# The three-pass products of two MLP-style mixings: float32r parts replaced by scaled float16 parts, with a range check and a second path

## The chip, the cores and the metric

The kernel runs on one core of a Trainium2 chip. The metric is the device time of one execution in microseconds (us); lower is better. Three runs of the kernel before gave 607.79, 611.24 and 612.61 us, median 611.24 us. The profile that is read below is one further execution.

## The reference

`B, H, S, D = 2, 8, 768, 64`, so 1536 rows of 512 columns, in 12 tiles of 128 rows. Causal windowed attention (8 global keys, a window of 96, a distance bias) gives `x`; then two mixings follow. The MLP weights reach the kernel as float64.

```python
attn_out = _attn_ref(**attn_kwargs)                  # softmax(q k / 8 + bias, masked) v
x = ascontiguousarray(attn_out.transpose(0, 2, 1, 3)).reshape(B, S, H * D)
# first mixing: layer norm, 512 -> 2048 -> 512
xn = (x - mu) / np.sqrt(var + 1e-06) * g_ln
x = x + np.maximum(xn @ w_ch1, 0.0) @ w_ch2
# second mixing: along the 768 rows (768 -> 256 -> 768), then 512 -> 1536 -> 512
u = x + (np.maximum(x.transpose(0, 2, 1) @ w_tok1, 0.0) @ w_tok2).transpose(0, 2, 1)
out = u + np.maximum(u @ w_ch1, 0.0) @ w_ch2
```

## The kernel before

**Products in three passes.** Every product of the mixings is made from a high and a low part of each operand: `hi` is the operand rounded to the matmul's type (ScalarE, `hi_lo`, L312, or `Weights.split`, L630), `lo` is the rest (VectorE, L316 and L319, or GpSimd and VectorE, L633). `mm3` (L323 to L326) then adds hi·hi, hi·lo and lo·hi in PSUM. The parts are float32r, a 4-byte type; PSUM is float32. Matmuls of the attention itself use float32 and, from tile 6 on, 16-bit parts (`ph`, `pl` float16 against `vb` bfloat16, L449 to L451).

**Tiling.** Rows go in four groups of three tiles (`xa`, `xb`, `u`). A first-layer block (tile `L1`, shown as `L`) is 4 chunks of 128 rows of weights times 3 passes, 12 matmuls of 384 columns; a second-layer block (`L2`, `L2S`) adds 4 or 2 hidden blocks, 12 or 6 matmuls of 512 columns; the product along the rows (`tok1`, `tok2`) has 512 columns. In the later part the first layer uses a Strassen-like scheme (`Factors`, `summands`, `pair`): sums and differences of weights (`Q`, then split into `sz`) and of activations (`K`, `V`, then split into `t`, `u`) are made on VectorE and GpSimd, and seven products stand for eight.

**Weights.** `Weights.get` loads 512 KB of float64 words into `stg`, ScalarE makes the sign and exponent word `fw` (L603), VectorE joins it with the mantissa (L614) in PSUM (`conv`) or SBUF (`wf`), then the two parts are split. Weights of both mixings are stored split in device memory (`scr_...`, 512 KB each) and loaded again for later groups.

**Order.** All engines' programs are written out by a planner (`Plan.order`): each operation has an engine, a cost and a due time, and a simulated list scheduler gives the order; buffers are pools with fixed counts (`SIZES`). Tables of letters (`LOA1`, `SE`, `FE`, ...) say which engine does which low part or sum; tables of numbers (`SLOT`, `LEAD`, ...) shift due times.

**Branches and end.** `setup_consts` computes a flag (the two counts fit the windowed path, L84); every engine loads it (L1202) and branches: windowed path, or `Else` with the general path. Behind it SyncE stores the last two tiles (`BEHIND`, `store`, L934).

Of the kernel before, what the change touches and what calls it, by code (L numbers as in the profile page):

```python
# [22 lines left out]
P = 128  # L23
# [11 lines left out]

class Ctx:
# [3 lines left out]
def setup_consts(o, tp):  # L40
# [17 lines left out]
    for fw in o.fws:  # L58
        nc.gpsimd.memset(fw[:, :, 0], 0.0)
# [8 lines left out]
    nc.scalar.activation(out=warm[:], in_=o.mhalf, func=AF.Exp)  # L68

# [5 lines left out]
                                   op1=ALU.add)  # L75
    ps = o.nps.tile([P, 2], F32, name="nps")
# [3 lines left out]
    flag = cp.tile([1, 1], I32, name="flag")  # L80
# [3 lines left out]
    nc.vector.scalar_tensor_tensor(out=flag[:], in0=ng, scalar=float(NGF), in1=c2[:, 1:2], op0=ALU.is_le, op1=ALU.mult)  # L84
# [444 lines left out]
def norm_ops(o, plan, prio, T, grp, i):  # L529
# [4 lines left out]
    xn = Buf("xn", lambda: o.ln.tile([P, C], F32, tag="xn", name="xn", bufs=1))  # L534
# [32 lines left out]

class Weights:


    def __init__(self, o, plan, keep):
        self.o, self.plan, self.kept, self.keep = o, plan, set(), keep

    def get(self, src, prio):
# [3 lines left out]
        b = Buf(key, lambda: o.wp.tile([P, 2, 512], F32R, tag=key, name=key))  # L578
        if src in self.kept:
            op("S", 1.46, prio - RELOAD, lambda: o.nc.sync.dma_start(b.t[:].bitcast(F32), o.kept[src][:]), r=[("kept", src)],  # L580
               w=[(b, "h"), (b, "l")], get=[b])
            return b
        self.split(src, prio, lambda: (b.t[:, 0, :], b.t[:, 1, :]), (b,), [b])
        if src[0] in self.keep:
            def store():
                t = o.kept[src] = o.scr.tile([P, 2, 512], F32, name=f"scr_{src[0]}{src[1]}{src[2]}")
                o.nc.sync.dma_start(t[:], b.t[:].bitcast(F32))
            op("S", 1.46, prio + STORE, store, r=[(b, "h"), (b, "l")], w=[("kept", src)])
            self.kept.add(src)
        return b  # L590

    def split(self, src, prio, dst, key, get=(), r=(), after=()):
        o, nc, op = self.o, self.o.nc, self.plan.op
        engs = {(1, "a"): LOA1, (1, "b"): LOB1, (2, "a"): LOA2, (2, "b"): LOB2}.get(src[:2], LOT)
        lo_eng = engs[src[2]] if o.w64 else "G"
        stg = Buf("stg", lambda: next(o.stg))
        if o.w64:
            if src in o.staged:
                op("N", LOADED[src], -9.0 + 0.1 * src[2], lambda: None, w=[(stg, 0)], get=[stg])
# [3 lines left out]
            op("A", 0.57, prio - 2, lambda: nc.scalar.activation(  # L603
                out=fw.t[:, :, 1], in_=stg.t[:, 4:2049:4].bitcast(BF16), func=AF.Copy),
# [21 lines left out]
        def shaped():  # L626
# [24 lines left out]
class Factors:  # L651
# [4 lines left out]
    def __init__(self, o, plan, name, xs, tiles, prio, r=(), after=()):  # L656
# [5 lines left out]
        for j in range(2):  # L662
            sx = [Buf("sx", lambda: next(o.sx)) for _ in range(4)]

            for z, (x, kc, k) in enumerate(((xa, j, ka), (xb, j, kb), (xa, 2 + j, ka), (xb, 2 + j, kb))):
                self.sum(op, nc, FE[z], prio, lambda z=z, sx=sx: sx[z].t, lambda x=x, kc=kc: x()[:, 0, kc, :n].bitcast(F32),
                         lambda x=x, kc=kc: x()[:, 1, kc, :n].bitcast(F32), ALU.add, n, r=[*k, *r], w=[(sx[z], 0)], get=[sx[z]])
# [3 lines left out]
            for i, z in enumerate((0, 3, 1, 2)):  # L671
# [4 lines left out]
                         lambda i=i, j=j: self.tiles()[i][:, 0, j].bitcast(F32), ALU.subtract, n,  # L676
# [11 lines left out]
def mlp_ops(o, plan, W, groups, blocks, which, t0, stores=False, lead=8.0, factors=None):  # L688
# [18 lines left out]
    def hidden():  # L707
        return Buf("hid", lambda: o.hid.tile([P, 2, max(GROUPS) * P], F32R, tag="h", name="h"))

    def l1(bi, f, g):  # L710
# [12 lines left out]
        cost = 12 * (0.014 + n / 2400)  # L723
# [7 lines left out]
    def l2(bi, hs, fs, g, ti, end, use="L2"):  # L731
# [12 lines left out]
        op("T", 3 * len(fs) * 0.227, prio, fn, r=keys, w=[(b, 0)], get=[b])  # L744
# [4 lines left out]
        now[0] += 3 * len(fs) * 0.216  # L749

    def summands(bi, fs):
# [16 lines left out]
        for i in range(2):  # L768
# [4 lines left out]
                        lambda i=i: z[i].t[:, 0].bitcast(F32), ALU.subtract, 512, r=[*k, (z[i], "h")], w=[(z[i], "l")])  # L773
        return w, z

    def pair(bi, fs, gs, pending):
# [7 lines left out]
        cost = 6 * (0.014 + n / 2400)  # L784
# [79 lines left out]
def token_ops(o, plan, b, uT, prio):  # L864
# [388 lines left out]
```

## Time and profile before

| | |
|---|---|
| median of 3 runs | 611.24 us |
| profiled execution, own time | 609.82 us |
| its span (first to last instruction) | 607.8 us |
| TensorE matmul / weight load busy | 586.1 us (96%) / 516.8 us |
| VectorE / ScalarE / GpSimd busy | 451.7 / 255.5 / 160.4 us |
| moved by DMA | 118.54 MB, mean 195 GB/s |

Busy time of TensorE is modelled: a matmul's duration in the trace lasts until its result has left the array, so consecutive matmuls overlap, and what a stream costs is read from start to start, not from the mean duration. PEld is the weight load, a record of its own. The chain of waits tells which engine's work stood last at each moment.

### The profile page before, as it was taken

The numbers are of one execution on the slowest core, as the hardware profiler recorded it, in microseconds if no ns is written. First come the engines' busy times: TensorE is split into PE (matmuls) and PEld (weight loads), VectorE is DVE, ScalarE is ACT, GpSimd is POOL, SyncE is SP. The second block draws the span as 40 slices with busy tenths as digits, with TensorE's granted clock in tenths as the row PEclk, the third lists the DMA queues.
The fourth block names the chain that finished last, engine by engine and source line by source line (L and its number), as shares of the span: only waits on it lengthen the run. The fifth ranks groups of instructions, "written<-read, shape, count | busy, mean of one in ns | idle before, by whom it ended". The sixth has DMA issues, their size and how long they took to land.

```text
span 607.8 us, 9319 instructions
## 1 busy us (share of the span) xinstructions
PE 586.1 (96%) x3318; PEld 516.8 (85%) x3318; DVE 451.7 (74%) x974; ACT 255.5 (42%) x499; POOL 160.4 (26%) x159
## 2 busy tenths in 40 slices
PE   3989999999999899999999999999999999999997
PEld 3767988988988788999899988798999898999986
DVE  7777676677754687988778987685699999677642
ACT  5778663446444353454222444341645423222100
POOL 2324143111602323243112311023343224411000
PEclk9989999999999999999999999999999999999999
DMA  9879999778936512748433545020429757553241
GB/s 260 302 215 314 315 325 327 287 231 281 310 132 234 191 47 70 243 151 302 169 127 121 201 177 208 1 105 35 174 74 342 278 168 249 185 194 140 104 157 57
DMA packets 63403, 118.54 MB, mean 195 GB/s; under 512 B 21620, under 2 KB 35956, under 8 KB 63348
## 3 DMA queue, kind: packets, MB, share of 16 engines
q1 hardware_dynamic: 63346, 117.86, 57.0%
q8 instruction: 28, 0.46, 0.3%
q14 instruction: 27, 0.22, 0.1%
q10 hardware_dynamic: 2, 0.00, 0.0%
HBM read 84.93 MB, written 32.51 MB: 193 GB/s over the span
## 4 chain that ended last, share of the span: by engine, by line
PE 85%; DMA 4%; DVE 4%; ACT 3%; issue 1%; POOL 1%; SPq 0%; POOLq 0%; DVEq 0%; ACTq 0%
PE L L324 16%; PE L L326 16%; PE L L325 15%; PE L2S L324 7%; PE L2S L325 7%; PE L2S L326 7%; PE S L405 4%; PE T L431 3%; PE PV L436 2%; PE tok L324 2%; PE tok L326 2%; PE tok L325 2%; DMA stg<-in_moe_w_ch_dram 2%; DMA stg<-in_moe_w_tok_dram 1%; ACT fw L603 1%
## 5 line engine op out<-in xcount | busy, mean ns | idle before, releaser
L746 DVE TENSOR_TENSOR x<-L2S,x 128x512 f32<-128x512 f32 x93 | 63.8, 687 | 25.7 <-PE L2S L326 25.1
L324 PE MATMUL L2S<-wb,h 128*128 128x512 f32 x204 | 80.1, 393 | 1.0 <-DVE x L746 1.0
L326 PE MATMUL L2S<-wb,h 128*128 128x512 f32 x204 | 79.8, 391 | 0.0
L325 PE MATMUL L2S<-wb,h 128*128 128x512 f32 x204 | 79.8, 391 | 0.0
L603 ACT ACTIVATE fw<-stg 128x512 f16<-128x512 bf16 x62 | 49.0, 791 | 50.0 <-DMA stg<-in_moe_w_ch_dram 32.4
L316 DVE SCALAR_TENSOR_TENSOR h<-L,h 128x384 fp32r<-128x384 f32 x56 | 31.0, 554 | 30.3 <-ACT h L312 29.9
L324 PE MATMUL L<-wb,h 128*128 128x512 f32 x132 | 53.1, 403 | 0.0
L326 PE MATMUL L<-wb,h 128*128 128x512 f32 x132 | 51.7, 392 | 0.0
L325 PE MATMUL L<-wb,h 128*128 128x512 f32 x132 | 51.7, 391 | 0.0
L312 ACT ACTIVATE h<-L 128x384 fp32r<-128x384 f32 x56 | 27.4, 489 | 55.1 <-PE L L326 54.8
L426 ACT ACTIVATE ex<-ex,mn 128x256 f32<-128x256 f32 (+1 forms) x96 | 41.6, 482 | 18.6 <-DVE mn L421 18.5
L324 PE MATMUL L<-xa,wa 128*128 128x384 f32 x136 | 46.9, 345 | 0.0
L324 PEld LDWEIGHTS L2S<-wb,h 128*128 128x128 f32 x204 | 38.3, 188 | 9.3 <-DVE x L746 2.4
L326 PE MATMUL L<-xa,wa 128*128 128x384 f32 x136 | 45.7, 336 | 0.0
L746 DVE TENSOR_TENSOR x<-L,x 128x512 f32<-128x512 f32 x33 | 22.8, 690 | 30.9 <-PE L L326 30.7
L325 PE MATMUL L<-xa,wa 128*128 128x384 f32 x136 | 45.6, 336 | 0.0
L633 POOL TENSOR_TENSOR wb<-wf,wb 128x512 fp32r<-128x512 f32 x17 | 23.4, 1387 | 83.8 <-ACT wb L630 77.9
L326 PEld LDWEIGHTS L2S<-wb,h 128*128 128x128 f32 x204 | 38.3, 188 | 8.2
L325 PEld LDWEIGHTS L2S<-wb,h 128*128 128x128 f32 x204 | 38.4, 188 | 6.8
L421 DVE CUSTOM_DVE_ANT_0 ex<-bmh,S 128x256 f32<-128x256 bf16 (+1 forms) x96 | 34.0, 394 | 6.1 <-PE S L405 5.8
L312 ACT ACTIVATE h<-V 128x384 fp32r<-128x384 f32 x28 | 14.4, 523 | 55.0 <-DVE V L800 35.9
L633 POOL TENSOR_TENSOR wa<-wf,wa 128x512 fp32r<-128x512 f32 x14 | 18.7, 1333 | 66.9 <-ACT wa L630 65.3
(194 smaller groups left out, 1527.1 us busy)
## 6 DMA issues: line engine op xcount, KB each, us to landing
stg<-in_moe_w_ch_dram SPq DMA_DIRECT2D x56, 512.0 KB, 5.3
wa<-scr_1a SPq DMA_DIRECT2D x24, 512.0 KB, 4.3
wb<-scr_1b SPq DMA_DIRECT2D x24, 512.0 KB, 5.4
scr_1a<-wa SPq DMA_DIRECT2D x16, 512.0 KB, 4.1
scr_1b<-wb SPq DMA_DIRECT2D x16, 512.0 KB, 5.3
wa<-scr_2a SPq DMA_DIRECT2D x16, 512.0 KB, 3.5
wb<-scr_2b SPq DMA_DIRECT2D x16, 512.0 KB, 4.0
scr_2a<-wa SPq DMA_DIRECT2D x12, 512.0 KB, 2.6
```

The source lines that it names most:

```text
L312: nc.scalar.activation(out=hi(), in_=src(), func=AF.Relu if relu else AF.Copy)
L316: nc.vector.scalar_tensor_tensor(out=lo(), in0=src(), scalar=0.0, in1=hi().bitcast(F32), op0=ALU.max, op1=ALU.subtract)
L324: nc.tensor.matmul(ps, ah, bh, start=first, stop=False)
L325: nc.tensor.matmul(ps, ah, bl, start=False, stop=False)
L326: nc.tensor.matmul(ps, al, bh, start=False, stop=last)
L405: nc.tensor.matmul(bs[j].t[:, i, :w], o.Q[r, qs, p + i, :], o.K[r, slots, p + i, :], start=True, stop=True)
L421: nc.vector.tensor_tensor_reduce(out=ex.t[:, j, :w], in0=o.bmh[:, h, ms, :], in1=bs[j].t[:, p % 2, :w], scale=-0.125, scalar=1e30, op0=ALU ...
L426: nc.scalar.activation(out=ex.t[:, j, :w], in_=ex.t[:, j, :w], func=AF.Exp, bias=mn.t[:, h:h + 1], scale=-1.0)
L431: nc.tensor.transpose(bt.t[:, j, i, :], ex.t[:, j, i * P:(i + 1) * P], o.ident[:])
L603: op("A", 0.57, prio - 2, lambda: nc.scalar.activation(out=fw.t[:, :, 1], in_=stg.t[:, 4:2049:4].bitcast(BF16), func=AF.Copy), r=[(stg, 0) ...
L633: op(lo_eng, {"G": 1.26, "V": 0.6}[lo_eng], prio, lambda: eng.tensor_tensor(out=dst()[1], in0=shaped(), in1=dst()[0].bitcast(F32), op=ALU. ...
L746: op("V", 0.6, prio, lambda: nc.vector.tensor_tensor(out=x[:], in0=b.t[:], in1=x[:], op=ALU.add), r=[(b, 0)], w=xk(T))
```

## The change

All parts of the mixings become float16. First-layer and `tok1` weights are multiplied by 8 and second-layer and `tok2` weights by 256, and the results are multiplied back by 1/2048 as they are added to `x`. The edits that follow from it:

- the tiles of parts and the stored copies of the weights are half as large; the freed SBUF goes to more buffers (`hid`, `wa`, `wb` 5 to 8, `xz` 3 to 6, `sx` 8 to 12, `stg` 3 to 4, `fw` 2 to 3, `xn` 1 to 2);
- the low part of a weight that is scaled by 8 is one `scalar_tensor_tensor` and always on VectorE, where GpSimd did some;
- `Guard` checks ranges on chip: 86 ScalarE squares with a sum along the row (31 first-layer-like weights, 31 second-layer-like weights, 24 for `x`), 4 sums that come with the ReLU of `tok1`, and one maximum of `g_ln` on VectorE; near the end they are compared with limits, with a small matmul that tests float16's smallest numbers, and give a second flag, `again`;
- `If/Else` becomes two `If`s: behind the windowed path every engine loads `again` and branches over the general path (float32r, as before) unless it is set;
- the tables of letters and numbers are new, and the planner's matmul costs are lower.

```diff
-        b = Buf(key, lambda: o.wp.tile([P, 2, 512], F32R, tag=key, name=key))
+        b = Buf(key, lambda: o.wp.tile([P, 2, 512], o.dt, tag=key, name=key))
...
+            if o.half and src not in self.seen:
+                self.seen.add(src)
+                o.guard.square("first" if src[1] == "a" else "second", prio, lambda: b.t[:, 0, :], [(b, "h")])
...
-                t = o.kept[src] = o.scr.tile([P, 2, 512], F32, name=f"scr_{src[0]}{src[1]}{src[2]}")
+                t = o.kept[src] = o.scr.tile([P, 2, 512], F16 if o.half else F32, name=f"scr_{src[0]}{src[1]}{src[2]}")
...
+        wide = o.half and (src[1] == "b" or src[0] == "tok2")
+        fine = o.half and not wide
+        scale = W3 if fine else W8 if wide and not o.w64 else 1.0
...
-        lo_eng = engs[src[2]] if o.w64 else "G"
+        lo_eng = "V" if scale != 1.0 else engs[src[2]] if o.w64 else "G"
...
+            op("V", 0.6, prio, lambda: nc.vector.scalar_tensor_tensor(
+                out=dst()[1], in0=shaped(), scalar=scale, in1=plain(dst()[0]), op0=ALU.mult, op1=ALU.subtract),
...
-        op("V", 0.6, prio, lambda: nc.vector.tensor_tensor(out=x[:], in0=b.t[:], in1=x[:], op=ALU.add), r=[(b, 0)], w=xk(T))
+        op("V", 0.6, prio, lambda: nc.vector.scalar_tensor_tensor(
+            out=x[:], in0=b.t[:], scalar=BACK if o.half else 1.0, in1=x[:], op0=ALU.mult, op1=ALU.add), r=[(b, 0)], w=xk(T))
...
+    AT = {"first": (0, 31, 8.0, 256.0), "second": (31, 62, 8.0, 2.0 ** 24), "x": (62, 86, 8.0, 2.0 ** 16),
+          "z": (86, 90, 0.0, 60000.0), "g": (90, 91, 0.125, 16.0)}
...
+    def square(self, kind, prio, src, r):
+        c, k = self.col(kind)
...
+            o.nc.scalar.activation(out=junk, in_=y, func=AF.Square, accum_out=c)
+        self.plan.op("A", 0.65, prio, fn, r=r, w=[k])
...
-LOA2 = 'GGGGVGGVGGVV'
+LOA2 = 'GGGVGVVGGVGG'
...
-FE, SE = 'VVVVVVGVGVVG', 'VGVVGVGV'
+FE, SE = 'GGGVVVVVGGVV', 'VGVGVGVV'
...
-    with tc.If(near != 0) as cmp:
+    o.half, o.dt = True, F16
+    with tc.If(near != 0):
         with ExitStack() as c2, tc.manual_schedule():
             rest_pools(o, c2)
             rest(o, c2, WindowAttention(o), True)
-    with cmp.Else():
+    again = nc.values_load(o.again[0:1, 0:1], min_val=0, max_val=1)
+    o.half, o.dt, o.staged = False, F32R, []
+    with tc.If(again != 0):
```

Three places show how rows move. On TensorE, the first product of the first mixing (`L_...` is its PSUM tile, `xa` the activations, `wa` the weights) stands before as

```order
L324 MATMUL L_696<-xa,wa 128x384
L325 MATMUL L_696<-xa,wa 128x384
L326 MATMUL L_696<-xa,wa 128x384
L324 MATMUL L_696<-xa,wa 128x384
L325 MATMUL L_696<-xa,wa 128x384
```

and in the changed kernel as

```order
L338 LDWEIGHTS wa
L338 MATMUL L_719<-xa,wa 128x384
L339 LDWEIGHTS wa
L339 MATMUL L_719<-xa,wa 128x384
L340 LDWEIGHTS wa
L340 MATMUL L_719<-xa,wa 128x384
```

The number and the shapes of the matmuls stay; the weight load, which a 4-byte matmul carries with it, is an instruction of its own for 16-bit operands.

On GpSimd, in the part with Strassen-like products, the rows before are sums of weights (L684, `Q`), their low parts (`sz`) and low parts of weights (L633, `wa`, `wb`):

```order
L684 TENSOR_TENSOR sz<-Q,sz 128x512
L633 TENSOR_TENSOR wa<-wf,wa 128x512
L684 TENSOR_TENSOR Q<-wa 128x512
L684 TENSOR_TENSOR Q<-Q 128x256
L633 TENSOR_TENSOR wa<-wf,wa 128x512
L684 TENSOR_TENSOR sz<-Q,sz 128x512
L633 TENSOR_TENSOR wa<-wf,wa 128x512
L633 TENSOR_TENSOR wb<-wf,wb 128x512
```

and now, with more of the sums of activations (`sx`, `K`) and without `sz` and `wa`:

```order
L777 TENSOR_TENSOR Q<-Q 128x256 x2
L723 TENSOR_TENSOR wb<-wf,wb 128x512
L777 TENSOR_TENSOR sx_2983<-u_2987 128x384
L777 TENSOR_TENSOR sx_2984<-u_2988 128x384
L777 TENSOR_TENSOR sx_2985<-u_2987 128x384
L777 TENSOR_TENSOR Q<-wa 128x512
L777 TENSOR_TENSOR Q<-Q 128x256
L777 TENSOR_TENSOR K<-u_2987 128x384
```

The 14 low parts of `wa` and the 14 of `sz` that GpSimd made are VectorE's now; 14 of VectorE's `Q<-Q` sums and 12 of its sums for `Factors` are GpSimd's.

On VectorE, the end of the windowed path (`x_74`, `x_75` are the last two tiles) was

```order
L316 SCALAR_TENSOR_TENSOR h<-L_6068,h 128x384
L316 SCALAR_TENSOR_TENSOR h<-L_6084,h 128x384
L746 TENSOR_TENSOR x_73<-L_6102,x_73 128x512
L746 TENSOR_TENSOR x_74<-L_6115,x_74 128x512
L746 TENSOR_TENSOR x_75<-L_6130,x_75 128x512
L1203 UNCONDITIONAL_BRANCH
```

and is now

```order
L839 SCALAR_TENSOR_TENSOR x_73<-L_6233,x_73 128x512
L839 SCALAR_TENSOR_TENSOR x_74<-L_6246,x_74 128x512
L839 SCALAR_TENSOR_TENSOR x_75<-L_6261,x_75 128x512
L1327 UNCONDITIONAL_BRANCH x2
L1331 TENSOR_LOAD flags
L1333 COMPARE_AND_BRANCH
```

The load of the second flag and a second branch stand between the last addition and the program's end; SyncE has the same rows between the stores of tiles 6 to 9 and those of tiles 10 and 11. VectorE writes the flag 21 rows earlier, ahead of the last products.

## Rows read from the trace of the kernel before

**Rows 1.** The page: busy us (share) xinstructions; the chain's shares by engine
```profile
PE 586.1 (96%) x3318; PEld 516.8 (85%) x3318; DVE 451.7 (74%) x974; ACT 255.5 (42%) x499; POOL 160.4 (26%) x159
...
PE 85%; DMA 4%; DVE 4%; ACT 3%; issue 1%; POOL 1%; SPq 0%; POOLq 0%; DVEq 0%; ACTq 0%
```
**Rows 2.** By stretch: length; PE, PEld, DVE, ACT, POOL busy (count); PEclk, DMA share, GB/s
```profile
0.00:60.00 60.00, 46.06 (x304) 37.28 (x304) 44.57 (x159) 42.62 (x91) 19.18 (x38) 0.97 0.86 272
60.00:435.00 375.00, 371.48 (x2176) 327.79 (x2176) 277.75 (x586) 160.26 (x310) 98.76 (x86) 1.00 0.56 189
435.00:510.00 75.00, 75.00 (x376) 67.37 (x375) 69.63 (x127) 32.88 (x64) 27.86 (x23) 1.00 0.63 223
```
**Rows 3.** The same over the span: line L324; tile h on PE; tile tok
```profile
0.00:608.00 608.00, 296.92 (x804) 151.13 (x804) 1.00 0.57 195
...
0.00:608.00 608.00, 242.69 (x1008) 1.00 0.57 195
...
0.00:608.00 608.00, 36.40 (x144) 26.42 (x144) 11.03 (x16) 2.36 (x4) 1.00 0.57 195
```
**Rows 4.** Timeline of PE near the end: start us, us, engine, line, operation
```profile
588.97 0.33 PE L324 MATMUL L<-xb,wa 128*128 128x384 f32 x1
...
595.24 0.39 PE L324 MATMUL L<-wb,h 128*128 128x512 f32 x1
...
603.21 0.39 PE L326 MATMUL L<-wb,h 128*128 128x512 f32 x1
```
**Rows 5.** Timeline of PE, a group of 16-bit matmuls and the one behind
```profile
98.45 0.22 PE L451 MATMUL PV<-vb,pl 128*128 128x130 bf16 x1
...
98.89 0.22 PE L451 MATMUL PV<-vb,pl 128*128 128x130 bf16 x1
98.92 0.48 PE L324 MATMUL L<-wb,h 128*128 128x512 f32 x1
99.23 0.39 PE L325 MATMUL L<-wb,h 128*128 128x512 f32 x1
```
**Rows 6.** Groups by line and shape: count, busy us, mean ns, idle before; weight loads
```profile
L324 PEld LDWEIGHTS L2S<-wb,h 128*128 128x128 f32 x204 | 38.3, 188 | 9.3 <-DVE x L746 2.4
L449 PEld LDWEIGHTS <-ph 128*128 128x128 f16 x88 | 8.5, 97 | 2.4 <-issue 2.0 <-ACT wb L630 0.3 <-ACT ex L426 0.2
```
**Rows 7.** Groups by line and shape: first and second pass of one product
```profile
L324 PE MATMUL L<-wb,h 128*128 128x512 f32 x132 | 53.1, 403 | 0.0
L325 PE MATMUL L<-wb,h 128*128 128x512 f32 x132 | 51.7, 391 | 0.0
```
**Rows 8.** Groups by line and shape: low parts and sums on DVE
```profile
L633 DVE TENSOR_TENSOR wa<-conv,wa 128x512 fp32r<-128x512 f32 x14 | 9.6, 688 | 5.5 <-ACT wa L630 5.5
L684 DVE TENSOR_TENSOR sz<-Q,sz 128x512 fp32r<-128x512 f32 x14 | 10.7, 764 | 0.0
L684 DVE TENSOR_TENSOR Q<-Q 128x256 f32<-128x256 f32 x42 | 19.2, 457 | 4.1 <-POOL Q L684 3.8
L684 DVE TENSOR_TENSOR K<-K 128x384 f32<-128x384 f32 x9 | 4.9, 548 | 0.0
```
**Rows 9.** Groups by line and shape: a ScalarE pass over 512 columns in SBUF
```profile
L312 ACT ACTIVATE xs<-x 128x512 fp32r<-128x512 f32 x12 | 7.3, 624 | 3.2 <-PE tok L326 3.2
```
**Rows 10.** Timeline of SP and DVE at the end: stores of tiles 9, 10, 11
```profile
598.91 0.33 SPq L934 DMA_DIRECT2D out_dram<-x  x1
...
600.92 0.69 DVE L746 TENSOR_TENSOR x<-L,x 128x512 f32<-128x512 f32 x1 [2.03 <-PE L L326]
602.23 2.46 SPq L934 DMA_DIRECT2D out_dram<-x  x2
603.63 0.69 DVE L746 TENSOR_TENSOR x<-L,x 128x512 f32<-128x512 f32 x1 [2.02 <-PE L L326]
```
**Rows 11.** Timeline at the start: the first flag, and the first work behind its branch
```profile
5.16 0.15 DVE L84 SCALAR_TENSOR_TENSOR flag<-nval,c 1x1 int32<-1x1 f32 x1
...
6.02 0.25 POOL L1078 MEMSET vb<- 128x24 bf16 x1 [2.18 <-DVE both L86]
```

More of the change, by code (lines that the diff above doesn't have):

```diff
@@ L75, in setup_consts @@
                                    op1=ALU.add)
+    nc.gpsimd.memset(o.again, 1)
     ps = o.nps.tile([P, 2], F32, name="nps")
@@ L79, in setup_consts @@
     c2 = tp.tile([1, 2], F32, name="c2")
-    flag = cp.tile([1, 1], I32, name="flag")
+    flag = o.flag
     ng, nl = nval[:, 0, :], nval[:, 1, :]
@@ L874, in token_ops @@
         op("A", 0.52, pr, h, r=[*xk(T), ("tk",)], w=[(xs, "h")], get=[xs])
+        if o.half:
+            o.guard.square("x", pr + GUARDX, lambda T=T: o.x[T][:], xk(T))
         op("V", 0.6, pr, l, r=[*xk(T), (xs, "h")], w=[(xs, "l")], lock=True)
@@ L940, in rest_pools @@
     o.xnp = pool("xnp")
-    o.hid = pool("hid", SIZES["hid"])
-    o.wp = pool("wp", SIZES["wa"])
-    o.wf = pool("wf", SIZES["wf"])
-    o.stg = cycle(o.stgs)
-    o.fw = cycle(o.fws)
+    o.sizes = SIZES if o.half else WIDE
+    o.hid = pool("hid", o.sizes["hid"])
+    o.wp = pool("wp", o.sizes["wa"])
+    o.wf = pool("wf", o.sizes["wf"])
+    more = [o.xnp.tile([P, 2050], U16, name=f"stg{i}") for i in range(o.sizes["stg"] - len(o.stgs))]
+    o.stg = cycle(o.stgs + [y[:] for y in more])
+    more = [o.xnp.tile([P, 512, 2], F16, name=f"fw{i}") for i in range(len(o.fws), o.sizes["fw"])]
+    for y in more:
+        tc.nc.scalar.memzero(y[:])
+    o.fw = cycle(o.fws + more)
     o.ln = pool("ln", 2)
     o.scr = pool("scr", 1, space=bass.MemoryType.DRAM)
-    o.ps = {p: pool("ps" + p, SIZES[p], space=PSUM) for p in PSUMS}
+    o.gp = pool("gp")
+    o.ps = {p: pool("ps" + p, o.sizes[p], space=PSUM) for p in PSUMS}
     o.kept = {}
@@ L1022, in rest @@
                 ("t1", j), r=[("tk",)])
+        if fast:
+            o.guard.square("first", t2 + TOKW + 4 * j + GUARDX, lambda j=j: o.t1[:, 0, 2 * j:2 * j + 2, :], [("t1", j, "h")])
     for j in range(3):
@@ L1026, in rest @@
                 r=[("tk",)])
+        if fast:
+            o.guard.square("second", t2 + TOKW + 12 + 4 * j + GUARDX, lambda sl=sl: o.t2[:, 0, :, sl], [("t2", j, "h")])
     uT = {}
@@ L1049, in rest @@
         free = [x for i in fac.keys for k in i for x in plan.readers.get(k, ())]
+    c, k = o.guard.col("g")
+    plan.op("V", 0.6, t2 + GUARDX, lambda: nc.vector.tensor_reduce(out=c, in_=o.gB[:], op=ALU.max, axis=AX.X, apply_absolute_value=True),
+            r=[("gB",)], w=[k])
+    o.guard.end(t - 30.0)
     plan.emit()
@@ L1194, in mixer_kernel @@
     o.V = o.cp.tile([P, 3, H, D + 1], F32, name="V")
-    stg = o.cp.tile([P, SIZES["stg"], 2050], U16, name="stg")
-    o.stgs = [stg[:, i, :] for i in range(SIZES["stg"])]
-    o.fws = [o.cp.tile([P, 512, 2], F16, name=f"fw{i}") for i in range(SIZES["fw"])]
+    stg = o.cp.tile([P, WIDE["stg"], 2050], U16, name="stg")
+    o.stgs = [stg[:, i, :] for i in range(WIDE["stg"])]
+    o.fws = [o.cp.tile([P, 512, 2], F16, name=f"fw{i}") for i in range(WIDE["fw"])]
     o.x = [o.cp.tile([P, C], F32, name=f"x{T}") for T in range(NTT)]
     o.staged = []
+    flags = o.cp.tile([1, 2], I32, name="flags")
+    o.flag, o.again = flags[:, 0:1], flags[:, 1:2]
     with tc.tile_pool(name="mtmp", bufs=1) as tp, tc.tile_pool(name="nps", bufs=1, space=PSUM) as o.nps, tc.manual_schedule():
```

202 lines of the change are left out of this document (138 added, 64 removed).

## The prediction

> **What bounds the kernel now.** I read the page first, then busy time by stretch, then start times. TensorE is busy for 586.1 us of the span, VectorE for 451.7, and the chain of waits lies on TensorE for 85% [rows 1]. By stretch, TensorE has all its idle time at the two ends: of the first 60 us it works 46.1, from 60 to 435 us it works 371.5 of 375, from 435 to 510 us all 75 [rows 2]. So from 60 us on the time is that of TensorE's stream, and what counts is the distance from one matmul's start to the next. The second engine to watch is VectorE between 435 and 510 us: 69.6 of 75 us [rows 2].
>
> The stream is nearly all three-pass products. Line L324 issues 804 first passes [rows 3], so there are 3 x 804 = 2412 matmuls. Of these, 1008 with `h` as weights and 144 into `tok` have 512 columns [rows 3], 1152 together, and the other 1260 have 384. Starts give the steps: 36 matmuls of 384 columns from 588.97 to 595.24 us make 174.2 ns each, and 35 steps of 512 columns from 595.24 to 603.21 us make 227.7 ns [rows 4]. The granted clock is 1.00 outside the first 60 us [rows 2], the 2.4 GHz level, at which 384 and 512 columns alone take 160.0 and 213.3 ns. Each float32r matmul thus carries about 14.3 ns that are not columns.
>
> **The change, part by part.** *Steps.* The trace of before has 16-bit matmuls, in the attention's last product. Three groups of 130, 64 and 130 columns pass between the starts at 98.45 and 98.89 us [rows 5]: 146.7 ns for a group of 324 columns, which alone take 135.0. That leaves 3.9 ns a matmul, and each of them has its own weight load. I take 3.9 ns for the wide ones too: 217.2 ns for 512 columns and 163.9 for 384. Saved are 10.5 ns x 1152 = 12.1 us and 10.3 ns x 1260 = 13.0 us, together 25.1 us. No row shows a 16-bit matmul wider than 130 columns, so the ends are 0 (14.3 ns stay) and 34.5 us (nothing but columns: 14.4 x 1152 + 14.2 x 1260).
>
> One rule speaks against a gain here. The Trainium skill, "TensorE: Matmul & The Clock Gate", section "Wait — 56ns, not 53.3ns?", gives columns / 2.4 GHz plus about 2.5 ns as the start-to-start distance of warm matmuls, 215.7 ns at 512 columns, and names no operand type. If it held for float32r, before would stand at 215.7 ns already and nothing could be won; the rows have 227.7. For the 16-bit group it fits better, 2.5 against 3.9 ns, and with it the two savings would be 28.2 us instead of 25.1.
>
> *First pass of a group.* The first float32r matmul behind other work is late: 0.31 us from 98.92 to 99.23 us against 0.228 [rows 5]. A float32r weight load takes 188 ns, a float16 one 97 [rows 6], so a short matmul ahead hides the latter more easily. The first pass of `L<-wb,h` is busy 1.4 us longer than the second over 132 products [rows 7]; were it so for all 804, 8.5 us could be won. Most products follow another of their kind, so I take 3 us; the ends are 0 and 8.5.
>
> *Work that changes engine.* VectorE takes 14 low parts of `wa` (0.688 us each) and 14 of `sz` (0.764) from GpSimd, and gives it 14 `Q` sums (0.457) and 12 sums for `Factors` (0.548) [rows 8]: 9.6 + 10.7 - 6.4 - 6.6 = 7.3 us more. Where it is 93% busy, in the stretch from 435 to 510 us, TensorE's 75 us shrink to 75 x 217.2 / 227.7 = 71.5 us. The second mixing's `wa` had 8 low parts on GpSimd, 8 x 0.688 = 5.5 us on top of VectorE's 69.6, or 75.1 us in 71.5. Against this, eight instead of five weight buffers and twelve instead of eight for sums let that work be done earlier, where VectorE has 97 us free (60 to 435 us [rows 2]). I take 2 us of new waits, ends 0 and 6 (the whole 3.6, and three of `sz`'s parts).
>
> *Checks.* 86 squares of a 128x512 tile go to ScalarE; the nearest row is a pass over 512 columns in SBUF, 0.624 us [rows 9], so 53.7 us. ScalarE is busy for 255.5 us [rows 1] and would be for some 309 of 585. Its queue is in order, so a high part behind a square comes up to 0.62 us later, and the low part and the product behind that; a product of 12 matmuls lasts 12 x 0.217 = 2.6 us and eight hidden buffers are filled ahead, which covers it. I take 0. With the cover gone in six places it would be 4 us.
>
> *Transfers.* Stored copies are half as large. From 60 us on DMA is busy to 0.56 [rows 2] and TensorE does not wait, so this is worth 0 there. In the first 60 us it is busy to 0.86 with 13.9 us of TensorE idle [rows 2], most of which belongs to the first attention tiles, that the change leaves alone but orders anew. I take 0, ends 4 us either way.
>
> *The end.* SyncE had issued tile 9's store by 599.24 us and issued tile 10's at 602.23, though its addition had ended at 601.61 [rows 10]: 3.0 us for the branch over the general path. Now a flag load and a second branch stand there. At the start, 0.7 us pass from the flag (5.31 us) to the first work behind load and branch (6.02) [rows 11]. If the added jump is short and costs nothing, SyncE is ready 0.7 us later, at 602.9 us of before's time, still ahead of tile 11's addition (ends 604.32); VectorE, which must also leave before the program ends, is later by the load and by the wait for its jump. I take 1 us, ends 0 and 3.7 (load and one full jump in a row).
>
> *Additions to `x`* become one instruction of the same size with a factor: 0, VectorE's slack covers a few ns each.
>
> **The sum**, against the profiled execution's own 609.8 us (its span is 607.8): 609.8 - 25.1 - 3 + 2 + 0 + 0 + 1 = 584.7 us. The median of the runs shown, 611.24, is 1.4 us above this execution; I predict **585 us**.
>
> **Rivals.**
>
> *VectorE becomes the bound* from 435 us on. For it: 93% busy there and more work in less time. Against: its whole sum rises by only 7.3 of 451.7 us, the buffers grow, and TensorE waited nowhere in this stretch. If the 3.6 us and as much again in the other Strassen stretches are paid on top, it is 592 us. It decides where VectorE's work of a stretch exceeds TensorE's.
>
> *The step does not shorten*: the 14.3 ns are those of any wide matmul. For it: no wide 16-bit row. Against: 130 columns with 3.9 ns. 609.8 + 2 + 1 = 613 us, no change.
>
> *Weight loads stop hiding*, now that they are instructions of their own. Were each 97 ns [rows 6] added to its matmul, steps would be 314 and 261 ns, which is 86.6 ns x 2412 = 209 us more than before: 819 us. Against it: the 16-bit groups have a load for every matmul and still run at 146.7 ns for three, less than two loads. The Trainium skill, same page, section "The mechanism", says that a weight load overlaps running matmuls only when it goes to other rows of the array, which would make this come true; the 16-bit rows don't agree with it.
>
> *The other side: the general path runs.* One check that fails sets `again`, and everything is done a second time. No row shows a value. From the reference's scales, a first-layer weight row has 512 x (8 / sqrt 512)² = 64 in limits of 8 and 256, a second-layer one 512 x (256 / sqrt 2048)² = 16384 between 8 and 2^24, both far from an edge; open is the test with float16's smallest numbers, which fails if TensorE or a conversion drops them. The general path's program has 1344 matmuls of 384 columns and 1152 of 512: 1344 x 0.174 + 1152 x 0.228 = 496 us on TensorE alone, so at least 1081 us. A single failing column decides it.
>
> **How the numbers follow.** Forecast 0.77 (own range 575 to 593 us); VectorE as the bound 0.12 (588 to 600); no shorter step 0.05; weight loads 0.01; general path 0.05. A measurement of this kernel can tell about 1% from no change, 6 us. The first two cases are faster by more than that: with a little taken off for mishaps, 0.88; same 0.06; slower 0.06. For 8 times in 10 the range leaves out the last three cases and the edges of the first two: 575 to 598 us. Its low end has the saving of 34.5 us, its high end 6 us of VectorE and 3.7 us at the end on top of a saving of some 20.
>
> **What would show it.** Starts of 512-column matmuls 217 ns apart and of 384-column ones 164 (right) or 228 and 174 (wrong). First and second passes busy alike. No instruction of the general path. TensorE idle between 60 us and the end below 6 us; more, released by VectorE's low parts of `wa`, `h` or `sz`, makes the second case. Last addition to the last instruction: 3.4 us before, 4 to 5 now. The forecast is wrong if the steps stay, or if TensorE's idle time grows by over 10 us.

## The result, and the profile after

| | before | changed |
|---|---|---|
| median | 611.28 us (607.79 to 612.61) | 571.45 us (570.04 to 572.78, 4 runs) |
| ratio to before | | 0.9357, 95% interval 0.9317 to 0.9397 |
| profiled execution, own time / span | 609.82 / 607.8 us | 572.36 / 570.5 us |
| moved by DMA | 118.54 MB | 82.90 MB |

The change takes 6.4% off, 40 us. The forecast was 585 us with a range from 575 to 598: right in direction, but the gain was half as large again as the sum said, and the time lies below the low end of the range.

The page of the changed kernel (columns as in [rows 1] and [rows 7]; the chain's shares are the line that begins with PE 85%):

```profile
span 570.5 us, 9478 instructions
...
PE 552.5 (97%) x3323; PEld 320.5 (56%) x3323; DVE 438.2 (77%) x965; ACT 319.9 (56%) x702; POOL 140.6 (25%) x168
...
PE 85%; DVE 7%; DMA 3%; ACT 1%; issue 1%; SPq 0%; ACTq 0%; DVEq 0%
...
L338 PE MATMUL L2S<-wb,h 128*128 128x512 f16 x204 | 77.3, 379 | 1.0 <-DVE x L839 1.0
...
L338 PEld LDWEIGHTS <-h 128*128 128x128 f16 x336 | 33.0, 98 | 36.9 <-issue 1.0
...
L338 PE MATMUL L<-wb,h 128*128 128x512 f16 x132 | 50.1, 379 | 0.0
L340 PE MATMUL L<-wb,h 128*128 128x512 f16 x132 | 50.0, 379 | 0.0
L339 PE MATMUL L<-wb,h 128*128 128x512 f16 x132 | 50.0, 379 | 0.0
```

TensorE is still the bound. A weight load takes 98 ns instead of 188 [rows 6], and the first pass (L338) is now as long as the other two, where it was 12 ns longer [rows 7]. ScalarE is busy for 64 us more, the checks, VectorE for 13 us less. By stretch, shorter now because everything comes earlier (columns as in [rows 2]):

```profile
0.00:60.00 60.00, 51.05 (x344) 40.81 (x345) 45.19 (x169) 48.35 (x104) 16.70 (x48) 1.00 0.80 241
60.00:400.00 340.00, 339.21 (x2113) 195.18 (x2112) 265.75 (x567) 205.99 (x452) 88.94 (x85) 1.00 0.48 154
400.00:475.00 75.00, 74.75 (x403) 39.36 (x401) 69.05 (x123) 41.83 (x94) 26.23 (x25) 1.00 0.39 127
475.00:571.00 96.00, 87.50 (x469) 45.20 (x466) 58.25 (x109) 23.73 (x53) 8.71 (x10) 0.97 0.22 70
```

In the first 60 us TensorE works 51.05 us instead of 46.06 [rows 2]. From 60 to 475 us its idle time is 1.0 us, although VectorE is at 69 of 75 us at the end of it, as it was before.

The timeline of TensorE at the place of [rows 4], the last first-layer block of 36 matmuls and the last second-layer block of 36, and then VectorE and SyncE behind it:

```profile
548.71 0.33 PE L338 MATMUL L<-xb,wa 128*128 128x384 f16 x1
...
554.56 0.38 PE L338 MATMUL L<-wb,h 128*128 128x512 f16 x1
...
562.12 0.38 PE L340 MATMUL L<-wb,h 128*128 128x512 f16 x1
562.53 0.69 DVE L839 SCALAR_TENSOR_TENSOR x<-L,x 128x512 f32<-128x512 f32 x1 [1.90 <-PE L L340]
566.30 1.05 SPq L1036 DMA_DIRECT2D out_dram<-x  x2
```

36 steps of 384 columns take 5.85 us, 162.5 ns each; 35 of 512 take 7.56 us, 216.0 ns. Before it was 174.2 and 227.7. The rows of SyncE show the price of the new end: the last addition is over at 563.22 us, but the two last stores are issued only at 566.30 us, and the span ends 7.3 us behind the addition. Before, tile 11's addition ended at 604.32 us [rows 10] and the span at 607.8, 3.4 us.

What TensorE waited for, between 60 us and its end, by the view of waits (us in total, times, longest); before, then the changed kernel:

```profile
PE norm L517 <- POOL xn L559: 1.7, 1, 1.7
PE L2S L324 <- DVE x L746: 1.0, 2, 0.6
PE tok L324 <- DVE u L319: 0.4, 1, 0.4
PE uT L517 <- DVE x L898: 0.3, 1, 0.3
```

```profile
PE L2S L338 <- DVE x L839: 1.0, 3, 0.4
```

**Where the 37.3 us of span went.** From all starts in the two traces (wide: of a three-pass product; step: the mean distance from one wide matmul to the next, without the long ones; late: what a first wide matmul behind other work costs beyond its own step and that of the work ahead; stalls: distances behind a wide matmul that are over 60 ns too long, whether the next one is wide or of other work):

| term | before | after | difference | forecast |
|---|---|---|---|---|
| first start of TensorE | 4.8 us | 3.7 us | -1.1 | 0 |
| 1152 steps of 512 columns | 228.8 ns | 215.9 ns | -14.9 | -12.1 |
| 1260 steps of 384 columns | 175.1 ns | 162.5 ns | -15.9 | -13.0 |
| late first matmuls | 4.2 us | 1.6 us | -2.6 | -3 |
| stalls behind wide matmuls | 5.4 us | 2.9 us | -2.4 | +2 |
| the rest: attention, transposes, waits among them | | | -4.2 | 0 |
| last matmul's start to the span's end | 4.6 us | 8.4 us | +3.8 | +1 |

Between two wide matmuls the stalls stay (2.1 and 2.0 us); what falls are those ahead of other work, 3.3 to 1.0. Counted by time, with one usual distance for each shape of matmul, TensorE loses 17.6 us beyond these distances in the first 60 us before and 13.4 after, and behind 60 us 6.4 and 1.3.

### The profile page after: what moved, and what is told of

It reads as the page before. It is cut to its first block, busy times and chain, and to the rows that moved or that the text cites. A ratio compares the mean times of both kernels' runs of the same rounds, so it can differ in the third digit from the quotient of the medians.

```text
span 570.5 us, 9478 instructions
## 1 busy us (share of the span) xinstructions
PE 552.5 (97%) x3323; PEld 320.5 (56%) x3323; DVE 438.2 (77%) x965; ACT 319.9 (56%) x702; POOL 140.6 (25%) x168
## 2 busy tenths in 40 slices
DMA packets 63405, 82.90 MB, mean 145 GB/s; under 512 B 21620, under 2 KB 35956, under 8 KB 63348
## 4 chain that ended last, share of the span: by engine, by line
PE 85%; DVE 7%; DMA 3%; ACT 1%; issue 1%; SPq 0%; ACTq 0%; DVEq 0%
PE L L338 15%; PE L L340 15%; PE L L339 15%; PE L2S L338 6%; PE L2S L340 6%; PE L2S L339 6%; PE S L419 4%; PE PV L450 4%; PE T L445 4%; DVE x L839 2%; PE tok L339 2%; PE tok L338 2%; PE tok L340 2%; DMA V<-in_v_dram 2%; DVE h L330 1%; PE norm L531 1%
## 5 line engine op out<-in xcount | busy, mean ns | idle before, releaser
L338 PE MATMUL L2S<-wb,h 128*128 128x512 f16 x204 | 77.3, 379 | 1.0 <-DVE x L839 1.0
L340 PE MATMUL L2S<-wb,h 128*128 128x512 f16 x204 | 77.3, 379 | 0.0
L339 PE MATMUL L2S<-wb,h 128*128 128x512 f16 x204 | 77.3, 379 | 0.0
L839 DVE SCALAR_TENSOR_TENSOR x<-L2S,x 128x512 f32<-128x512 f32 x93 | 63.7, 687 | 15.1 <-PE L2S L340 14.7
L330 DVE SCALAR_TENSOR_TENSOR h<-L,h 128x384 f16<-128x384 f32 x56 | 31.1, 555 | 32.3 <-ACT h L324 32.1
L340 PEld LDWEIGHTS <-h 128*128 128x128 f16 x336 | 32.9, 98 | 39.7
L339 PEld LDWEIGHTS <-h 128*128 128x128 f16 x336 | 32.9, 98 | 37.9 <-issue 2.8
L338 PEld LDWEIGHTS <-h 128*128 128x128 f16 x336 | 33.0, 98 | 36.9 <-issue 1.0
L324 ACT ACTIVATE h<-L 128x384 f16<-128x384 f32 x56 | 27.3, 487 | 45.2 <-PE L L340 44.9
L338 PE MATMUL L<-wb,h 128*128 128x512 f16 x132 | 50.1, 379 | 0.0
L340 PE MATMUL L<-wb,h 128*128 128x512 f16 x132 | 50.0, 379 | 0.0
L339 PE MATMUL L<-wb,h 128*128 128x512 f16 x132 | 50.0, 379 | 0.0
L839 DVE SCALAR_TENSOR_TENSOR x<-L,x 128x512 f32<-128x512 f32 x33 | 22.7, 689 | 29.2 <-PE L L340 29.2
L338 PE MATMUL L<-xa,wa 128*128 128x384 f16 x136 | 44.4, 326 | 0.0
L340 PE MATMUL L<-xa,wa 128*128 128x384 f16 x136 | 44.3, 326 | 0.0
L339 PE MATMUL L<-xa,wa 128*128 128x384 f16 x136 | 44.3, 326 | 0.0
L338 PEld LDWEIGHTS <-wa 128*128 128x128 f16 x308 | 30.2, 98 | 21.2 <-issue 1.0
L339 PEld LDWEIGHTS <-wa 128*128 128x128 f16 x308 | 30.1, 98 | 20.2
L340 PEld LDWEIGHTS <-wa 128*128 128x128 f16 x308 | 30.1, 98 | 19.9
```

The lines of the kernel that those rows point to most:

```text
L338: nc.tensor.matmul(ps, ah, bh, start=first, stop=False)
L339: nc.tensor.matmul(ps, ah, bl, start=False, stop=False)
L340: nc.tensor.matmul(ps, al, bh, start=False, stop=last)
L839: op("V", 0.6, prio, lambda: nc.vector.scalar_tensor_tensor(out=x[:], in0=b.t[:], scalar=BACK if o.half else 1.0, in1=x[:], op0=ALU.mult, ...
```

## The experiments

Theory A: nearly all of it is the stream of matmuls; the step is a matter of the operand's type alone, and the rest comes from the new order. Rivals: the larger buffers and new tables do a good part (B); the checks cost something that the gain hides (C); VectorE is close to being the bound (D); the long float32r step is that of its long weight load, or of VectorE's traffic beside it (E).

**Float16 alone.** The order of before on every engine, with its tables, buffer counts, planner's costs and `Else`; only the parts are float16 (all weights by 256), and there are no checks. Against the changed kernel, without the tables:

```diff
-BACK = 1 / (W8 * W3)
+BACK = 1 / (W8 * W8)
...
-        wide = o.half and (src[1] == "b" or src[0] == "tok2")
+        wide = o.half
...
-    o.sizes = SIZES if o.half else WIDE
+    o.sizes = WIDE
...
-    o.guard = Guard(o, plan) if fast else None
+    o.guard = None
```

> Float16 parts alone, in the order of the kernel before on every engine (its tables, its buffer counts, its planner costs, its If/Else, no checks; every weight is scaled by 256 so that the low parts stay on the engines that made them). Theory stream: the trace of the changed kernel has 2.5 ns a matmul over its columns where before has 15.2, and no late first matmul behind other work (54 x 0.1 us before), so this run alone saves 2412 x 12.7 ns + 5.5 us = 36 us: about 575 us (572 to 579). Theory buffers and tables: the steps give the 25 us that were forecast and the new order and buffers the other 13: about 586 us.

577.27 us (576.73 to 577.75), ratio 0.9457 (0.9427 to 0.9486), 33.2 us less than the 610.42 of before on the same chip. From start to start it has the steps of the changed kernel, 215.8 and 162.5 ns, which is 30.8 us; late first matmuls and stalls, as in the table above, give 4.7 more, and the start and the attention take some 3 back. Its busy times in the first two stretches of [rows 2]:

```profile
0.00:60.00 60.00, 49.00 (x296) 39.10 (x296) 44.57 (x157) 41.46 (x88) 17.18 (x37) 0.97 0.77 232
60.00:435.00 375.00, 372.59 (x2309) 214.81 (x2309) 293.98 (x624) 173.77 (x338) 105.88 (x97) 1.00 0.44 139
```

Between 60 and 435 us TensorE gets through 2309 matmuls where before it was 2176 [rows 2], in the same order and with as few waits. The theory's 575 us (572 to 579) held: A has five sixths of the gain.

**And the larger buffers**, still in the old tables of numbers:

```diff
-    o.sizes = WIDE
+    o.sizes = SIZES if o.half else WIDE
```

> As f16_alone, with the larger buffer counts of the changed kernel, still with the tables of before. Theory stream: TensorE waits little in f16_alone already, so within 2 us of it. Theory buffers and tables: at least 4 us below f16_alone.

583.3 us (581.35 to 585.24), ratio 0.9544 (0.9511 to 0.9577): 6 us slower than without them. Both expectations missed. With more buffers the planner writes another order; in it TensorE waits, in the first 60 us, 9.2 us for ScalarE's exponentials (4.6 us in the kernel with float16 alone), and between 40 and 60 us it is granted 0.59 of its clock, for most of that time 1.2 GHz, the lower of its two levels. By stretch, and by waits:

```profile
40.00:60.00 20.00, 16.62 (x73) 13.09 (x72) 11.56 (x37) 12.81 (x24) 8.73 (x9) 0.59 0.59 188
```

```profile
PE T L444 <- ACT ex L439: 9.2, 5, 4.1
```

So the larger buffers by themselves are no gain. The new tables with the old buffer counts were not run.

**The changed kernel without checks and with `Else`** (`o.guard = None`, no `again`, one branch):

```diff
-    with tc.If(near != 0):
+    with tc.If(near != 0) as cmp:
...
-    again = nc.values_load(o.again[0:1, 0:1], min_val=0, max_val=1)
-    o.half, o.dt, o.staged = False, F32R, []
-    with tc.If(again != 0):
+    with cmp.Else():
+        o.half, o.dt, o.staged = False, F32R, []
```

> The changed kernel without its range checks (no squares, no sums, no second flag) and with the If/Else of before, so with the new tables, scales and buffers. Theory stream: the tables are worth the 1 us of an earlier start and some 3 us of waits, and the end is that of before (4.2 us behind the last matmul instead of 8.0): 567 us. Theory checks: ScalarE's 54 us of squares cost TensorE waits, 563 us or less here.

572.53 us (570.47 to 575.45), ratio 0.9394 (0.9354 to 0.9434). Both figures (567, and 563 or less) missed: nothing is gained by leaving the checks out. The order is another one without them, so times alone don't settle it; the trace of the changed kernel does. Its first square starts at 54 us, and from 60 us on TensorE waits 1.0 us in all, so from there on the checks can cost no more than that. C falls, except for what the checks do to the planner's order. Against float16 with the larger buffers the new tables are worth 10.8 us, against float16 alone 4.7, and that is what B has of the 40 us. The end is as short as before: last addition over at 565.37 us, span 568.7. The changed kernel's end is 4 us longer, and it has these back in the first 60 us, where TensorE works 51.05 us against 48.20 here.

**Without checks, but with the second flag and branch** (flag 0 from the start):

```diff
-    nc.gpsimd.memset(o.again, 1)
+    nc.gpsimd.memset(o.again, 0)
...
-    o.guard = Guard(o, plan) if fast else None
+    o.guard = None
```

> The changed kernel without the squares and the test of their sums; flag, second load and second branch stay, and the flag is 0 from the start. Theory (checks are hidden, the end costs 4 to 5 us): 571 to 572 us, the same as with checks, and 8 us from the last matmul's end to the end of the span. Rival (checks cost some us and the second branch little): 566 or less.

576.81 us (575.65 to 579.92), ratio 0.9483 (0.9441 to 0.9525): above both expectations, 4 us above the version with one branch and 5 us above the changed kernel with its checks (5 and 8 by the ratios; the chips differ). So here too leaving the checks out gains nothing. The order on TensorE is that of the version with one branch; the spans of the two profiled executions differ by 5.1 us, of which the longer end is 3.8. Against the changed kernel the loss lies at the start: TensorE works 46.4 us of the first 60 instead of 51.05, in the other order that the planner writes without the squares:

```profile
0.00:60.00 60.00, 46.39 (x323) 36.16 (x324) 43.75 (x164) 45.85 (x98) 16.22 (x36) 1.00 0.85 253
```

**Stores of the last two tiles inside the first branch:**

```diff
-BEHIND = (10, 11)
+BEHIND = ()
```

> The changed kernel with the stores of the last two tiles inside the windowed path, ahead of the second flag's load and branch. Theory end: the stores wait for VectorE to pass the second branch (3.0 us from its branch to its next record), so they go out 3.5 us earlier: 568 us. Rival: the engines' own branches set the last instruction anyway, and the time is within 1 us of the changed kernel, 571 us.

572.48 us (569.66 to 574.85), ratio 0.9362 (0.9325 to 0.9399): no gain, as the rival said. The last store is issued at once, but then SyncE itself has load and jump ahead of it, and the span (573.1 us) ends 6.1 us behind the addition (over at 566.93 us) instead of 7.3. Timeline of the end:

```profile
566.24 0.69 DVE L839 SCALAR_TENSOR_TENSOR x<-L,x 128x512 f32<-128x512 f32 x1 [1.90 <-PE L L340]
566.96 0.33 SPq L1036 DMA_DIRECT2D out_dram<-x  x1
```

The edit stands at the end, and the order on TensorE is that of the changed kernel. Yet the starts differ. From 40 to 60 us, here and in the changed kernel:

```profile
40.00:60.00 20.00, 16.10 (x112) 13.07 (x113) 11.36 (x39) 13.45 (x29) 8.74 (x12) 0.91 0.65 202
```

```profile
40.00:60.00 20.00, 19.23 (x140) 14.83 (x141) 14.30 (x48) 17.18 (x36) 9.45 (x12) 1.00 0.84 247
```

So two executions of the same order can lie 3 us apart in their start, and what one trace shows of a start is no surer than that.

**The second branch in the kernel before**, first with a late write of the flag by VectorE (a new operation for the planner), then with the flag 0 from the start, which leaves the order of every engine as it was:

```diff
-    with tc.If(near != 0) as cmp:
+    with tc.If(near != 0):
...
-    with cmp.Else():
+    again = nc.values_load(o.again[0:1, 0:1], min_val=0, max_val=1)
+    o.staged = []
+    with tc.If(again != 0):
```

The first version's extra operation is

```diff
+    plan.op("V", 0.2, t - 30.0, lambda: nc.vector.memset(o.again, 0), w=[("again",)])
```

> The kernel before with a second flag (written 0 late by VectorE), its load on every engine and a second branch over the general path instead of the else. Theory (load plus second branch cost about 4 us behind the last addition): 614 to 615 us, and from the last addition's end to the end of the span 7 us instead of 3.4. Rival (what was gained elsewhere made the longer end of the changed kernel, the branch adds under 1 us): 611 to 612.

> The kernel before in its own order on every engine, with one thing added: a second flag (0 from the start), its load and a second branch over the general path instead of the else. Theory (the second branch costs some 4 us behind the last addition, and the rest of the 12 us that the run with two branches lost came from its other order in the first 60 us): 614 to 615.5 us, 7 to 8 us from the last matmul's end to the end of the span, and the stretch to 60 us as in the kernel before. Rival (the branch or the flag themselves cost 12 us, at the start too): 620 to 622.

The first gave 621.26 us (618.53 to 621.53), ratio 1.0181 (1.0138 to 1.0223), which is 11 us more and not 4; the second 614.65 us (614.25 to 615.6), ratio 1.0055 (1.0036 to 1.0075), 3.4 us more. The first 60 us of the first and of the second version, and the end of the second, whose span is 612.8 us:

```profile
0.00:60.00 60.00, 46.12 (x266) 38.04 (x267) 43.17 (x156) 39.50 (x83) 18.64 (x38) 0.92 0.87 272
```

```profile
0.00:60.00 60.00, 47.06 (x300) 38.71 (x302) 44.43 (x158) 41.08 (x88) 18.31 (x38) 0.97 0.86 265
```

```profile
604.86 0.69 DVE L747 TENSOR_TENSOR x<-L,x 128x512 f32<-128x512 f32 x1 [2.03 <-PE L L327]
608.46 1.25 SPq L935 DMA_DIRECT2D out_dram<-x  x2
```

In the old order the second branch costs what the theory said: the addition is over at 605.55 us, the store issued 2.9 us later, the span ends 7.3 us behind the addition, 3.9 more than before. The rest of the first version's loss, some 7 us (6.8 between the two spans, 7.7 by the ratios), is its order: 266 matmuls in the first 60 us instead of 300 to 304, at a granted clock of 0.92. One added operation of 0.2 us in the planner moves the time by more than the branch does.

**More work on VectorE** in the changed kernel, one maximum over a constant tile behind every low part of the second mixing's weights:

```diff
+        if o.half and src[0] == 2:
+            op("V", 0.69, prio, lambda: o.nc.vector.tensor_reduce(out=o.minus[:, 2:3], in_=o.gB[:], op=ALU.max, axis=AX.X, apply_absolute_value=True), r=[("gB",), (b, "l")], w=[("extra",)])
```

> The changed kernel with one more instruction of 0.68 us on VectorE (a maximum over a constant tile, read by nobody) behind every low part of the second mixing's weights, 20 of them, 13.6 us in all. Theory (VectorE is well away from being the bound, larger buffers let it run ahead): 571 to 574 us, TensorE's stalls under 5 us. Rival of the prediction (VectorE is the bound in the second mixing): where it was 69 of 75 us busy it has 6 us left, so half or more of the rest comes on top, 578 to 583 us.

570.62 us (569.57 to 571.88), ratio 0.9371 (0.9335 to 0.9407). There were 24 of them, not 20. Their group, and the narrow stretch:

```profile
L673 DVE TENSOR_REDUCE minus<-gB 128x1 f32<-128x512 f32 x24 | 16.3, 678 | 0.0
```

```profile
400.00:475.00 75.00, 74.88 (x403) 39.32 (x402) 72.66 (x132) 41.29 (x96) 27.67 (x27) 1.00 0.39 130
```

16.3 us more on VectorE cost nothing. From 400 to 475 us it is busy 72.66 of 75 us, and TensorE idles for 0.12. D falls. The time is that of the changed kernel within both intervals.

**The step by itself.** A kernel of bare streams of 48 matmuls each, on one set of tiles: float32r (`w4`, `m4`) with 512, 384 and 256 columns, then with 64 and 32 weight columns; float16 (`w2`, `m2`) with 512, 384 and 256; then transposes and six matmuls in turn, float32r (L69, L71) and float16 (L74, L76); and at the end the float32r and the float16 stream once more (L81 to L83, L86 to L88). VectorE has work of its own in the run, which depends on none of the streams.

```diff
+    for i in range(N):
+        nc.tensor.matmul(ps[:, :512], w(w4, i), m4[:, :512], start=True, stop=True)
+    for i in range(N):
+        nc.tensor.matmul(ps[:64, :512], w(w4, i, 64), m4[:, :512], start=True, stop=True)
+    for i in range(N):
+        nc.tensor.matmul(ps[:, :512], w(w2, i), m2[:, :512], start=True, stop=True)
```

> Leaves the whole mixer out: only streams of 48 like matmuls on one set of tiles, so its time is of no interest and only the starts are. Theory 1 (float32r's extra time belongs to its weight load, 188 ns long): float32r of 512 columns 227 ns a step, of 384 columns 174; with 64 weight columns the load is half as long and the step falls to about 220, with 32 to 216. Theory 2 (it belongs to the moving operand, so it grows with columns or is fixed): 227 with 64 and 32 weight columns too; with 256 columns 114 to 121. Float16: 215.8, 162.5 and 109.2 ns under both. Behind a group of transposes the first float32r matmul is some 0.1 us late, the first float16 one under 0.02 us. If VectorE's work beside it were what slows float32r in the kernel, the bare stream would take 216 ns and the stream with VectorE's work 228.

Its timeline, consecutive instructions of a line together (start us, us from the first start to the last end):

```profile
18.64 11.04 PE L50 MATMUL ps<-m,w 128*128 128x512 f32 x48
29.52 8.51 PE L52 MATMUL ps<-m,w 128*128 128x384 f32 x48
37.87 5.91 PE L54 MATMUL ps<-m,w 128*128 128x256 f32 x48
43.61 11.20 PE L56 MATMUL ps<-m,w 128*64 128x512 f32 x48
54.65 11.28 PE L58 MATMUL ps<-m,w 128*32 128x512 f32 x48
65.77 10.53 PE L60 MATMUL ps<-m,w 128*128 128x512 f16 x48
76.14 7.96 PE L62 MATMUL ps<-m,w 128*128 128x384 f16 x48
83.94 5.40 PE L64 MATMUL ps<-m,w 128*128 128x256 f16 x48
...
101.64 0.60 PE L69 MATMUL pt<-ident,x 128*128 128x128 f32 x4
101.99 1.63 PE L71 MATMUL ps<-m,w 128*128 128x512 f32 x6
...
112.60 0.60 PE L69 MATMUL pt<-ident,x 128*128 128x128 f32 x4
...
116.15 0.60 PE L74 MATMUL pt<-ident,x 128*128 128x128 f32 x4
116.59 1.46 PE L76 MATMUL ps<-m,w 128*128 128x512 f16 x6
...
124.81 0.60 PE L74 MATMUL pt<-ident,x 128*128 128x128 f32 x4
```

One start to the next, over 48: float32r takes (29.52 - 18.64) / 48 = 226.7 ns at 512 columns, 174.0 at 384, 119.6 at 256, which is 13 to 14 ns over the columns whatever their number. With 64 and with 32 weight columns, whose loads are 134 and 109 ns long instead of 188, it is 230.0 and 231.7: no shorter, so theory 1 of this run falls. Float16 takes 216.0 and 162.5, 2.5 to 2.7 ns over the columns. VectorE's work fell beside the first streams, and beside the last ones there was none (columns as in [rows 2]):

```profile
18.64:29.50 10.86, 10.86 (x49) 9.01 (x48) 10.35 (x16) 0.00 (x0) 0.00 (x0) 1.00 0.01 2
```

```profile
128.00:149.00 21.00, 21.00 (x95) 17.36 (x93) 0.00 (x0) 0.00 (x0) 0.00 (x0) 1.00 0.00 1
```

The first of these stretches is the float32r stream of 226.7 ns, with VectorE at work for 10.35 of 10.86 us; in the second float32r takes 227 ns with VectorE idle. So its traffic is not the cause either. Float16 runs without VectorE here, and takes no longer in the changed kernel, where VectorE is 69 of 75 us busy (215.9 ns). E falls in both forms: the 13 to 14 ns go with each matmul of 4-byte operands, with neither the columns nor the load's length. One thing is left that no run separates from the operands' size: a 4-byte matmul carries its weight load with it, where float16 has an instruction for it. In the kernel before the average was 1 to 2 ns higher still, so of the 30.8 us the bare streams' steps give some 27; where the other 4 come from stays open.

Of the late first matmul little is left. Four transposes and six matmuls take (112.60 - 101.64) / 6 = 1.827 us with float32r and (124.81 - 116.15) / 5 = 1.732 with float16; the six steps account for 65 of the 95 ns (6 x 10.9), which leaves 30 ns a group, not 100. The float32r product is recorded as starting 0.35 us behind its first transpose, the float16 one 0.44: the former's start record comes 0.09 us early, and the "late" second start only makes up for it.

## Why the prediction was wrong, and where it was right

**The steps** had the right mechanism and too small a size: 30.8 us instead of 25.1. Two readings did it. "I take 3.9 ns for the wide ones too" carried over the mean of the three 16-bit matmuls of [rows 5]. In the trace it is the one of 64 columns that raises it: over all 88 groups it is followed after 32.8 ns, 6.1 over its columns, and the two of 130 columns after 56 to 57 (medians), 2 to 3 over. The wide ones have 2.5 (1.4 ns x 2412 = 3.4 us). And float32r's 227.7 and 174.2 came from one place near the end [rows 4], where the steps are shorter than the mean of 228.8 and 175.1 (2.4 us). The Trainium skill, "TensorE: Matmul & The Clock Gate", section "Wait — 56ns, not 53.3ns?", says columns / 2.4 GHz plus about 2.5 ns: for float16 the trace agrees to 0.2 ns (215.9 against 215.7), for float32r it does not (226.7 in the bare stream). The prediction had the saving by that rule, 28.2 us (28.4 by its own steps), and set it aside.

**New waits, +2,** had the wrong sign: from 60 us on TensorE's waits fell from 3.4 to 1.0 us (the two lists of waits above). "7.3 us more" of work on VectorE was in fact 13.5 us less: the list of work that changes engine had left out the letters for the attention's casts, copies and reductions. Groups of before that are gone from VectorE, or have 12 in place of 20 instructions now (`ao`):

```profile
L349 DVE CAST vb<-V 128x512 bf16<-128x512 f32 x12 | 6.4, 530 | 0.4 <-DMA V<-in_v_dram 0.4
...
L470 DVE COPY pt<-T 128x512 f32<-128x512 f32 x4 | 2.8, 691 | 0.3 <-PE T L431 0.3
...
L463 DVE TENSOR_REDUCE ao<-PV 128x130 f32<-128x260 f32 x20 | 8.2, 421 | 0.9 <-PE PV L451 0.9
```

These are 12 of the 21 us between the two figures. Nor was VectorE near a bound, as the 16.3 us of added work showed: a stretch that is 93% busy was read as almost late, though the low parts may be made long before they are needed. And the lower end of the term stood at 0, as if the waits that the trace of before has could not fall.

**Transfers and order, 0 with 4 either way,** was a blind spot about as large as what the steps fell short by: 5.3 us came off (first start, attention and transposes), and the runs show why no sign could be had from the diff. The new tables gave -4.7 us (against float16 alone), the buffers without them +6, one more planned operation in the kernel before some +7. Most of that is made in the first 60 us, which the prediction knew to hold 13.9 us of idle time [rows 2] and yet held to move by 4: counted as behind the table of terms, TensorE loses 17.6 us there before, 19.3 with float16 alone, 28.2 with the buffers, 15.1 with the new tables and 13.4 in the changed kernel, but 17.6 too in the changed kernel's order with the stores inside. So part of the 5.3 may be one execution's luck.

**First passes, -3,** came to -2.6. What [rows 5] show as 0.08 us of lateness is in part an early start record: the 16-bit matmul at 98.89 us is followed after 0.03 us where one of its size takes 0.057.

**The end, +1,** cost 3.8, just over the upper end that was given for it. "SyncE is ready 0.7 us later" and so ahead of the last addition's end was right: in the changed kernel it stands ready at 562.9 us. The step that failed is what was to follow from it: the stores wait for VectorE, whose load and jump lie behind the last addition. VectorE branches at 563.24 us and has its next record at 566.20, and the first of the two stores is issued at 566.30. In these 3 us two packets of the DMA queues for instructions start, at 563.65 and 564.29 us. The Trainium skill, "Runtime: NRT & Kernel Launch", section "Instruction fetch mechanics", says that a taken branch to a place that isn't prefetched waits for a DMA. The packets fit that, but no record says which engine they are for.

**Together.** The trace has 37.3 us of span less, the sum had 25.1. Of the 12.2 us between them the steps are 5.7, the start and the order 5.3 and the waits 4.4; the end takes 2.8 and the first passes 0.4 the other way. The sum of 584.7 us is for the profiled execution; for the median, 1.4 above it, it would have been 586, not 585.

**Right:** the checks at 0 (ScalarE rose by 64 us, and taking the checks out gained nothing); the weight loads stay hidden (98 ns each, beside steps that are columns plus 2.5 ns); no general path; and the additions with a factor cost nothing (687 ns each, as before).

**The range** failed for its own reason. Its low end, 575, is the largest saving on steps alone; the ends of the first passes (8.5 us) and of transfers (4 us) were not added below it, while at the high end several terms were. With them it would have reached some 563.

## What to carry to other kernels

When TensorE is the bound, read the step from a mean over the whole stream, not from one place, and a matmul of 16-bit operands as its columns at 2.4 GHz plus 2.5 ns (384 and 512 columns here, granted clock 1.00). A change that re-plans the order has a term of its own of some 5 us either way in a start that idles, which no diff sizes: it belongs in the range at both ends, and one trace tells it only to some 3 us. A second branch over a long path cost 3 to 4 us behind the last addition here, and moving the last stores ahead of it only moved the jump to another engine.

## What was not expected of the hardware

- Matmuls with 4-byte float32r operands carry 13 to 14 ns each beside their columns (226.7, 174.0 and 119.6 ns for 512, 384 and 256 columns), float16 ones 2.5; fewer weight columns do not help (230.0 ns with 64).
- A float16 weight load of 64 columns is longer than one of 128 (110 against 98 ns in the bare streams), while float32r's falls from 188 to 134. Their groups (columns as in [rows 6]):

```profile
L50 PEld LDWEIGHTS ps<-m,w 128*128 128x128 f32 x48 | 9.0, 188 | 1.9
...
L56 PEld LDWEIGHTS ps<-m,w 128*64 128x64 f32 x48 | 6.4, 134 | 4.4
...
L66 PEld LDWEIGHTS <-w 128*64 128x64 f16 x48 | 5.2, 110 | 5.1 <-issue 0.2
...
L60 PEld LDWEIGHTS <-w 128*128 128x128 f16 x48 | 4.6, 98 | 5.8 <-issue 0.4
```

- The start recorded for the first float32r matmul behind other work is some 0.09 us early, so single starts around a change of work mislead; periods over several groups do not (1.827 us with float32r against 1.732 with float16, of which the steps are 65 of the 95 ns).
